# Squared-ReLU attention and a mixture of adapters on Trainium2: another engine for most output stores, two engines for the last ones, and a new order of work

## The chip, the cores and the metric

The kernel runs on one core of one Trainium2 chip. The metric is the device time of a whole execution in microseconds (us); lower is better. The core has five engines that run beside each other, each through its own queue in order: TensorE (PE in the profile; its weight loads are PEld), VectorE (DVE), ScalarE (ACT), GpSimd (POOL) and SyncE (SP, which here only issues DMAs). DMAs can be issued from SP, ACT and POOL.

## What is computed

```python
# q, k, v: (8, 12, 448, 64) float32
scores = q @ k.transpose(0, 1, 3, 2) / sqrt(64)
attn   = maximum(scores, 0) ** 2 / 448
x      = (attn @ v) brought to (8*448, 12*64) = (3584, 768)
logits = x @ w_gate                       # 8 experts
w      = softmax over the 2 largest logits of a row
out    = x + sum over these 2 experts e of  w_e * (x @ A[e]) @ B[e]     # A: 768 x 16, B: 16 x 768
```

The output has 3584 rows of 768 float32. There is no softmax over the scores, so score blocks need no maximum and no sum: a ReLU and a square.

## The kernel before

**Attention.** The heads go in quads: for each of 8 batches there are 3 quads of 4 heads (`QUADS`, line 19), and for each quad 7 blocks of 64 keys (`J`), so 168 units `n` in all. For each batch and quad, `load` (line 291) brings q, k and v into SBUF by two GpSimd DMAs each, casting float32 to bfloat16; `tp` (413) transposes q and k on TensorE and copies them out of PSUM (line 437, DVE). For each unit, `qk` (492) makes the scores, `relu` (514) takes them out of PSUM (line 523 on ACT, 525 on DVE), `sq` (533) squares two or three units at once on DVE (541), and `pv` (548) multiplies by v (558). When the 7 blocks of a quad are summed, `xt_copy` (576) casts the result into `xt`, the transposed x (587).

**Adapters.** The 3584 rows are 28 tiles of 128. Tiles go through the gate in groups of mostly three: `gate` (596) multiplies by A and w_gate (604), finds the two largest logits, the weights and the weighted `zp` on DVE with a sigmoid on ACT (641), transposes `zp` on TensorE (665) and copies it to `zT` (674). `outputs` (704) then makes each tile in two halves of 384 columns: a float32 matmul `zT` by B (722) in PSUM, the x part added, and one evacuation per half into the tile's buffer `osb`. For tiles 15 to 25 x comes from SP's DMA transposes (`turned`, 683, issued at line 690, six for a group) and is added on DVE during the evacuation (752). For the other tiles x is added on TensorE (717) and the evacuation is a copy on ACT or DVE (757). `st` (765) stores a finished tile by two SP DMAs of 64 rows (771). `osb` has 4 buffers, so a tile can only be written when the store of the tile four places ahead of it has landed.

**The order.** Nothing here is a loop on the chip. The function `build` (254) makes a list of operations, each with an estimate of its duration, the engines it may run on and a rank; `schedule` (114) plays them through as a list scheduler, with the durations, latencies and buffer counts written in the file, and the instructions are emitted in the order of its start times. Three tables steer it: `C` (weights and latencies), `RANKS` (shifts of single operations by their number in the list) and `ENGINES` (operations tied to one engine). The `deps` of an operation steer this order only; the waits on the chip come from the tiles and buffers that the instructions read and write. `Dma.land` (106) is the planner's idea of when a load lands. DMAs of POOL use eight completion semaphores in turn, those of SP and ACT together another eight, and each DMA waits for the one that used its semaphore before.

**The start.** `first` (304) loads the first k as float32 by SP and ACT, a first part of three blocks (`raw`) and the rest (`raw_rest`, through `rest`, 327), and casts them on DVE (`k0` at 344, `k1` at 346). The first q comes by POOL.

Of the kernel before, what the change touches and what calls it, by code (L numbers as in the profile page):

```python
# [14 lines left out]
J = 7  # L15
# [9 lines left out]
ZW = RE + E  # L25

# [5 lines left out]
def parts(*cuts):  # L32
# [6 lines left out]
    out_=-0.80943, zt_=6.6019, a12=(4, 7), late=6, merge_x=0, id2=2.6063, ocap=3, tboth=1, sqs=(2, 2, 3), xback=(15, 24), xblat=3.0, xbdur=0.7,  # L39
    slack=0.097634, switch=3.9663, third=7.3082, dve_relu=0.18096, relu_until=400, qk=-2.3217, sq=10,  # L40
# [3 lines left out]
POOLS = dict(qT=5, a1=C["a12"][0], a2=C["a12"][1], zp=2, zT=3, osb=4, w=3, q=5, k=5, v=7, xb=4)  # L44
# [4 lines left out]
    0: 20, 85: 141, 113: -42, 122: -40, 142: -8, 144: 17, 147: -27, 148: 84, 154: -31, 167: -104, 168:  # L49
    -23, 180: 36, 189: 32, 195: -52, 196: -21, 199: 18, 215: 4, 216: 110, 217: 47, 220: -25, 222: 9, 225:  # L50
    10, 231: 10, 233: -54, 234: -43, 238: -65, 245: 62, 267: 90, 286: 1, 295: 11, 321: 84, 334: 180, 336:
    45, 341: -33, 351: 3, 356: -10, 359: -9, 373: 5, 409: 4, 414: -23, 417: -24, 432: -12, 446: 69, 447:
    57, 452: 33, 454: 46, 467: -47, 491: -15, 496: 3, 508: -22, 519: 57, 521: -6, 529: -4, 562: 110, 563:
    35, 568: -23, 573: 18, 607: 2, 612: 30, 627: 9, 642: 3, 649: 6, 662: -7, 667: 21, 694: 20, 723: 2,
    746: -26, 769: -19, 805: 3, 807: 20, 814: -78, 815: -77, 826: 46, 834: 52, 837: 15, 841: -41, 842:
    -14, 924: -12, 925: -15, 926: 66, 930: -11, 931: -12, 947: 137, 950: 127, 963: -11, 968: -13, 970:
    -63, 983: 59, 986: -28, 989: 141, 994: 45, 1001: -57, 1031: 123, 1034: 106, 1044: -71, 1050: -94,
    1056: 34,
}
ENGINES = {  # L60
    100: "ACT", 108: "ACT", 141: "ACT", 142: "ACT", 196: "ACT", 218: "DVE", 234: "ACT", 280: "ACT", 315:
    "ACT", 330: "ACT", 337: "ACT", 360: "ACT", 432: "ACT", 566: "DVE", 664: "DVE", 759: "ACT", 780:
    "ACT", 1011: "ACT", 1012: "ACT",
# [18 lines left out]
class Op:  # L82
    def __init__(self, engs, dur, fn, deps=(), after=None, mode=None, kind="", take=(), give=(),
                 rank=0.0, banks=None, free=(), lat=None, ni=0):
        self.engs, self.fn, self.mode, self.kind = engs, fn, mode, kind
        self.dur = dur if isinstance(dur, dict) else dict.fromkeys(engs, dur)
        self.lat, self.ni = lat, ni
        self.deps = [d for d in deps if d is not None]
        self.after = after
        self.take, self.give, self.rank = take, give, rank  # L90
        self.want, self.free, self.banks = banks, free, None
        self.start = self.end = self.eng = None
        self.users = []
        self.missing = len(self.deps) + (after is not None)
        self.ready = 0.0
        for d in self.deps + [after] * (after is not None):
            d.users.append(self)


class Dma:  # L100
# [5 lines left out]
    def land(self, t, o):  # L106
        if o.engs[0] != "POOL":
            return t + o.lat
        for x in (t - o.dur["POOL"] / 2, t):
            self.free = max(self.free, x + 0.5) + o.mb / 2 / (0.27 if 4.5 < self.free < 13 else 0.4)  # L110
        return self.free + (1.5 if self.free < 5 else 2.1 if self.free < 11 else 2.7)


def schedule(ops, c=C):
# [70 lines left out]
    while left:  # L185
# [9 lines left out]
        for e in free:  # L195
# [12 lines left out]
            if o.kind == "load":  # L208
                o.end = dma.land(free[e], o)
            else:  # L210
                o.end = free[e] + (LAT[e] if o.lat is None else o.lat)
# [42 lines left out]
def build(k=None, c=C):  # L254
# [36 lines left out]
    def load(b, w, q, deps):  # L291
        nm = "qkv"[w]

        def fn():
            t = new(nm, (nm, b, q), [128, 2, S], BF16)
            for g in range(2):
                nc.gpsimd.dma_start(out=t[g * PH : g * PH + PH],  # L297
                                    in_=k.qkv[w][b, g, :, 2 * q : 2 * q + 2, :])

        o = op(("POOL",), 1.17, fn, deps=deps, kind="load", take=(nm, "lane"), give=("lane",))  # L300
        o.mb = 4 * S * 64 * 4e-6
        return o

    def first():
# [30 lines left out]
        for d in ds:  # L335
# [5 lines left out]
        kr = [op((e,), 0.75, lambda g=g: rest(g), kind="load", rank=-48.0, lat=2.4, after=aw if g else None, deps=[ob],  # L341
                 to=more if g else ops)
              for g, e in enumerate(("SP", "ACT"))]
        k0 = op(DVE, dve(2 * CUT * PH, 1.92), lambda: nc.vector.tensor_copy(k.k_first, k.raw), deps=ds + [ob],
                rank=-50.0)
# [67 lines left out]
    def tp(b, q):  # L413
# [34 lines left out]
        if (b, q) == (0, 0):  # L448
# [24 lines left out]
            return [[e1, *es] + [e2] * (j >= CUT) for j in range(J)]  # L473
        m = op(PE, 0.225, lambda: mm(m, 0), deps=[loaded[b, w, q] for w in range(1 + c.get("tboth", 0))], mode="64",
# [16 lines left out]

    def qk(n):
        b, u, q, j = order[n]
        x0, x1 = PARTS[b][u]
        w = x1 - x0

        def fn():
            t = T["qT", b, q]
            for sl in range(2):
                r = slice(sl * PH, sl * PH + PH)  # L500
                at = 0 if sl else 512 - w
                for g in range(2):
                    nc.tensor.matmul(  # L503
                        out=bank(o, sl)[g * PH : g * PH + PH, at : at + w],
                        lhsT=t[r, g, 1, j * PH : j * PH + PH], rhs=t[r, g, 0, x0:x1],
                        start=True, stop=True,
                    )

        o = op(PE, w / 2400 + 0.005, fn, mode="64", kind="qk", ni=8, deps=tp_ops[b, q][j],
               after=qk_ops.get(n - 1), banks=("s", 2), give=("qT",) if n == last_use[b, q] else (),  # L510
               rank=n + at("qk", n))
        return o
# [35 lines left out]
    def pv(n):  # L548
# [4 lines left out]
        def fn():  # L553
            vn = T["v", b, q]
            for g in range(2):
                r = slice(g * PH, g * PH + PH)
                for sl in range(2):
                    nc.tensor.matmul(  # L558
                        out=bank(head, g)[sl * PH : sl * PH + PH, :w],
                        lhsT=vn[r, sl, j * PH : j * PH + PH],  # L560
                        rhs=T["a2", g0][r, i, sl * w : sl * w + w],
                        start=(j == 0), stop=(j == J - 1),
                    )
# [7 lines left out]
        o = op(PE, w / 2400 + 0.003, fn, mode="64", kind="pv", ni=8, deps=wait, after=pv_ops.get(n - 1),  # L571
# [111 lines left out]
    def turned(tiles):  # L683
# [10 lines left out]
        for q in range(QUADS):  # L694
            for g in range(2):
# [4 lines left out]
                            lat=c["xblat"], to=more)  # L700
        for t in tiles:
            xb_of[t] = [[ts[do] for do in range(3 * h, 3 * h + 3)] for h in range(2)], t0, tiles[-1]

    def outputs(tl):
# [60 lines left out]
        def st():  # L765
            r = 0
            while r < 128:
# [3 lines left out]
                nc.sync.dma_start(out=k.out[b, j, p : p + m], in_=T["osb", tl][r : r + m, :])  # L771
                r += m

        op(("SP",), 0.8, st, deps=evs, give=("osb",), kind="store", lat=2.5)
# [13 lines left out]
    for i in range(len(tiles_of) + 2):  # L788
# [5 lines left out]
        if i == 4:  # L794
            sel_op = op(("POOL",), 1.5, sel_fn)
            a_load = op(("POOL",), 1.5, aw_fn, kind="load")
            a_load.mb = 0.4
            b_load = op(("POOL",), 0.7, b_fn, kind="load")
            b_load.mb = 0.4
# [4 lines left out]
    while t < NT:  # L804
        m = min(c.get("gsz", 3), NT - t)
        if NT - t == 4:
            m = 2
        if t == NT - 2:
            m = 1
# [133 lines left out]
```

## Time and profile before

| | before |
|---|---|
| median of 5 runs | 184.98 us (184.11 to 186.82) |
| the profiled execution | 183.92 us |
| its span, first to last instruction | 182.2 us |
| busy in the span: PE / DVE / ACT / POOL | 165.2 / 164.5 / 155.1 / 88.7 us |
| granted TensorE clock, mean | 0.997 |
| TensorE, start of its last matmul | 175.66 us |
| last evacuation, start | 176.4 us |
| last store DMA, issued | 177.88 us |
| store DMAs of SP (line 771), x56, issue to landing, median | 3.5 us |
| transposes of SP (line 690), x24, one issue, median | 1.25 us |
| load DMAs of POOL (line 297), one issue, mean | 0.62 to 0.63 us |

The profile is one execution, recorded by the hardware. Times inside it count from its first instruction. "Busy" is the time in which an engine had an instruction running; DMA issues on SP and ACT do not count as busy. A wait names what ended it. The profiled execution took 1.7 us more than its span, which lies outside the first and last instruction.

### The profile page before, as it was taken

The page shows a single profiled execution, that of the slowest core. Times are in us where ns is not written, and L with a number is a line of the kernel's source. Part 1 is how long each engine was busy: PE and PEld are TensorE (multiplying, and loading weights), DVE is VectorE, ACT ScalarE, POOL GpSimd, SP SyncE. Part 2 cuts the span into 40 slices and gives each one's busy share as a digit, 9 for nine tenths or more (in the row PEclk, how much of TensorE's full clock was granted, in tenths as well). Part 3 has the DMA queues.
Part 4 walks back from the last instruction along what each step waited for, and adds up shares of the span by engine and source line. Part 5 has one row for each costly group of instructions (what it writes and reads, how often), then busy time and mean ns, then how long its engine had stood idle before and what let it go on. Part 6 is the DMA issues. An engine that isn't in the chain of part 4 may idle for free.

```text
span 182.2 us, 7403 instructions
## 1 busy us (share of the span) xinstructions
PE 165.2 (91%) x3186; PEld 96.4 (53%) x3186; DVE 164.5 (90%) x260; ACT 155.1 (85%) x225; POOL 88.7 (49%) x153
## 2 busy tenths in 40 slices
PE   7777889698999999999999999999999999999960
PEld 2434667355565556565565555655665454656530
DVE  1289999999999999999999999999999999999750
ACT  3399989999999999999999999999999999941100
POOL 7999869889897586736835743720000000000000
PEclk9999999999999999999999999999999999999998
DMA  4999999999999999995999999999563973744785
GB/s 98 180 174 160 187 188 149 183 185 179 173 167 203 239 236 242 241 191 96 184 164 169 221 191 166 171 134 193 115 166 66 133 187 67 187 103 101 191 262 171
DMA packets 36018, 31.02 MB, mean 170 GB/s; under 512 B 13648, under 2 KB 32336, under 8 KB 35984
## 3 DMA queue, kind: packets, MB, share of 16 engines
q0 software_dynamic: 21712, 16.90, 65.2%
q1 hardware_dynamic: 13984, 13.41, 30.0%
q8 instruction: 25, 0.41, 0.8%
q10 hardware_dynamic: 288, 0.23, 0.5%
q14 instruction: 9, 0.07, 0.2%
HBM read 33.84 MB, written 11.01 MB: 246 GB/s over the span
## 4 chain that ended last, share of the span: by engine, by line
PE 52%; ACT 26%; DVE 10%; issue 6%; DMA 2%; DVEq 0%; POOL 0%; ACTq 0%; POOLq 0%
ACT a L523 22%; PE ps L722 17%; PE ps L503 12%; PE ps L558 10%; DVE a L541 5%; PE ps L604 3%; PE ps L423 3%; PE ps L717 3%; DMA q<-in_q_dram 2%; DVE xt L587 2%; PE ps L375 2%; DVE qT L437 2%; ACT xt L587 1%; ACT osb L757 1%; PE ps L665 1%
## 5 line engine op out<-in xcount | busy, mean ns | idle before, releaser
L523 ACT ACTIVATE a<-ps 128x896 bf16<-128x896 f32 x159 | 136.6, 972 | 2.0 <-PE ps L503 1.8
L541 DVE TENSOR_TENSOR a<-a 128x1792 bf16<-128x1792 bf16 (+1 forms) x72 | 88.7, 1250 | 0.8 <-ACT a L523 0.7
L503 PE MATMUL ps<-qT 64*64 64x448 bf16 x672 | 60.0, 367 | 5.5 <-ACT a L523 3.8
L722 PE MATMUL ps<-B,zT 128*128 128x384 f32 x112 | 46.7, 512 | 0.1
L558 PE MATMUL ps<-a,v 64*64 64x448 bf16 x672 | 42.1, 350 | 1.4 <-ACT a L523 0.7
L503 PEld LDWEIGHTS <-qT 64*64 64x64 bf16 x672 | 24.0, 105 | 35.9 <-issue 27.1
L297 POOL DMA_DIRECT2D v<-in_v_dram x48 | 29.0, 619 | 21.1 <-PE ps L503 10.6
L297 POOL DMA_DIRECT2D q<-in_q_dram x48 | 29.4, 625 | 6.8 <-PE ps L423 2.1
L297 POOL DMA_DIRECT2D k<-in_k_dram x46 | 28.0, 630 | 3.3 <-PE ps L503 1.8
L558 PEld LDWEIGHTS <-v 64*64 64x64 bf16 x672 | 21.6, 106 | 11.8 <-issue 4.6
L437 DVE COPY qT<-ps 128x1792 bf16<-128x1792 bf16 x23 | 25.0, 1087 | 0.6 <-PE ps L423 0.4
L722 PEld LDWEIGHTS ps<-B,zT 128*128 128x128 f32 x112 | 17.6, 191 | 5.1 <-issue 1.0
L587 DVE CAST xt<-ps 128x448 bf16<-128x448 f32 x26 | 15.5, 622 | 0.9 <-PE ps L558 0.8
L604 PE MATMUL ps<-awg,xt 128*128 128x136 bf16 x168 | 13.4, 224 | 0.1
L423 PEld LDWEIGHTS <-q 64*64 64x64 bf16 x672 | 10.3, 111 | 4.8 <-issue 1.9
L604 PEld LDWEIGHTS <-xt 128*128 128x128 bf16 x168 | 10.2, 98 | 4.7 <-issue 4.0
L752 DVE TENSOR_TENSOR osb<-ps,xb 128x384 f32<-128x384 f32 x22 | 11.9, 556 | 0.8 <-DMA out_dram<-osb 0.4
L587 ACT CAST xt<-ps 128x448 bf16<-128x448 f32 x22 | 12.2, 590 | 0.3 <-PE ps L558 0.3
L717 PE MATMUL ps<-identb,xt 128*128 128x128 bf16 x102 | 11.5, 221 | 0.3 <-ACT a L523 0.2
L423 PE MATMUL ps<-identb,q 64*64 64x64 bf16 x672 | 10.0, 195 | 1.8 <-DMA q<-in_q_dram 1.3
L757 ACT COPY osb<-ps 128x384 f32<-128x384 f32 x22 | 11.5, 536 | 0.2
L717 PEld LDWEIGHTS <-xt 128*128 128x128 bf16 x102 | 6.6, 97 | 8.6 <-issue 7.7
(47 smaller groups left out, 95.7 us busy)
## 6 DMA issues: line engine op xcount, KB each, us to landing
out_dram<-osb SPq DMA_DIRECT2D x56, 192.0 KB, 3.5
q<-in_q_dram POOLq DMA_DIRECT2D x48, 112.0 KB, 4.9
v<-in_v_dram POOLq DMA_DIRECT2D x48, 112.0 KB, 5.0
k<-in_k_dram POOLq DMA_DIRECT2D x46, 112.0 KB, 5.1
B<-in_moe_B_dram POOLq DMA_DIRECT2D x1, 384.0 KB, 6.2
xb<-xt SPq DMA_TRANSPOSE x24, 2.9
a_raw<-in_moe_A_dram POOLq DMA_DIRECT2D x1, 192.0 KB, 5.0
raw_rest<-in_k_dram ACTq DMA_DIRECT2D x1, 128.0 KB, 4.6
```

The lines of the kernel that those rows point to most:

```text
L297: nc.gpsimd.dma_start(out=t[g * PH : g * PH + PH], in_=k.qkv[w][b, g, :, 2 * q : 2 * q + 2, :])
L423: nc.tensor.transpose(k.ps_b[sl * PH : sl * PH + PH, o.banks[g], (w * J + j) * PH : (w * J + j) * PH + PH], source(w, j)[r, sl], k.identb[ ...
L437: nc.vector.tensor_copy(t.rearrange("p g w x -> p g (w x)"), k.ps_b[:, m.banks[0] : m.banks[0] + 2, : 2 * S])
L503: nc.tensor.matmul(out=bank(o, sl)[g * PH : g * PH + PH, at : at + w], lhsT=t[r, g, 1, j * PH : j * PH + PH], rhs=t[r, g, 0, x0:x1], start ...
L523: nc.scalar.activation(out, flat(qk_ops[n], w), ACTF.Relu, scale=k.relu_scale)
L541: nc.vector.tensor_mul(a2, T["a1", g0], T["a1", g0])
L558: nc.tensor.matmul(out=bank(head, g)[sl * PH : sl * PH + PH, :w], lhsT=vn[r, sl, j * PH : j * PH + PH], rhs=T["a2", g0][r, i, sl * w : sl ...
L587: evac(w, lambda cp, g=g: cp(k.xt[:, g * QUADS + q, b * S + x0 : b * S + x1], bank(src, g)[:, :w]), deps=[pv_ops[n]], free=[(src, g)], ran ...
L604: nc.tensor.matmul(out=bank(zops[0])[:, t * ZW : t * ZW + ZW], lhsT=k.xt[:, do, 128 * tiles[t] : 128 * tiles[t] + 128], rhs=k.awg[:, do, : ...
L717: nc.tensor.matmul(out=out(h)[:, x * 128 : x * 128 + 128], lhsT=k.xt[:, 3 * h + x, c0 : c0 + 128], rhs=k.identb, start=(x == 0), stop=Fals ...
L722: nc.tensor.matmul(out=out(h)[:, :W], lhsT=T["zT", g0][:, zi], rhs=k.B[:, h * W : h * W + W], start=xb is not None, stop=True, skip_group_ ...
L757: cp(T["osb", tl][:, h * W : h * W + W], out(h)[:, :W])
```

## The change

- A table `STORES` gives the stores of tiles 6 to 22 to POOL and those of tiles 24 and 26 to ACT; the other tiles but the last stay with SP. The last tile, 27, is stored in halves of 384 columns: the first by SP once the first half is evacuated, the second by ACT after the second. A half takes two DMAs, as a whole tile did.
- The planner's operations for `raw_rest` (`kr`) depend on the cast `k0` and no longer on `ob`, and stand behind it in the list.
- The planner's numbers change: a tile's store 1.4 (POOL 1.05) where it was 0.8, a transpose 1.35 with latency 1.4 where it was 0.7 with 3.0; `Dma.land` now also models stores and transposes. `xb`, the transposed x, has 3 buffers where it had 4.
- `slack`, `switch`, `third` and `dve_relu` in `C` are new, and `RANKS` and `ENGINES` are replaced by other tables, so the order of all work is another.
- The k tile gets 64 more columns, and there are new functions `turn_qk` and `qk_turned` for batches from `bx` on. `bx` is 8 and there are 8 batches, 0 to 7, so they are never called, and the columns stay unused. `gl=(2, 1)` gives the group sizes that the code had.

```diff
+STORES = {**dict.fromkeys(range(6, 23), "POOL"), 24: "ACT", 26: "ACT"}
...
-    ..., xback=(15, 24), xblat=3.0, xbdur=0.7,
-    slack=0.097634, switch=3.9663, third=7.3082, dve_relu=0.18096, ...
+    ..., xback=(15, 24), xblat=1.4, xbdur=1.35, bx=8, gl=(2, 1), tqk=-25.0, tqlat=2.0,
+    slack=0.09816, switch=4.3786, third=6.0149, dve_relu=0.47201, ...
-POOLS = dict(..., v=7, xb=4)
+POOLS = dict(..., v=7, xb=3)
...
     def land(self, t, o):
+        if o.kind != "load":
+            self.free = max(self.free, t - o.dur[o.engs[0]] + 0.6) + o.mb
+            return max(self.free + 1.3, t + o.lat)
...
-        kr = [op((e,), 0.75, lambda g=g: rest(g), kind="load", rank=-48.0, lat=2.4, after=aw if g else None, deps=[ob],
+        k0 = op(DVE, dve(2 * CUT * PH, 1.92), lambda: nc.vector.tensor_copy(k.k_first, k.raw), deps=ds + [ob],
+                rank=-50.0)
+        kr = [op((e,), 0.75, lambda g=g: rest(g), kind="load", rank=-48.0, lat=1.6, after=aw if g else None, deps=[k0],
                  to=more if g else ops)
               for g, e in enumerate(("SP", "ACT"))]
-        k0 = op(DVE, dve(2 * CUT * PH, 1.92), lambda: nc.vector.tensor_copy(k.k_first, k.raw), deps=ds + [ob],
-                rank=-50.0)
...
-        def st():
+        def st(e, c1=0, c2=2 * W):
...
-                nc.sync.dma_start(out=k.out[b, j, p : p + m], in_=T["osb", tl][r : r + m, :])
+                {"SP": nc.sync, "ACT": nc.scalar, "POOL": nc.gpsimd}[e].dma_start(
+                    out=k.out[b, j, p : p + m, c1:c2], in_=T["osb", tl][r : r + m, c1:c2])
                 r += m
 
-        op(("SP",), 0.8, st, deps=evs, give=("osb",), kind="store", lat=2.5)
+        def store(e, es, **kw):
+            half = "fn" in kw
+            o = op((e,), 1.05 if e == "POOL" else 1.4, kw.pop("fn", lambda: st(e)), deps=es, kind="store", lat=1.9, **kw)
+            o.mb = (1.25 if e == "POOL" else 1.5) / (1 + half)
+
+        if tl < NT - 1:
+            store(STORES.get(tl, "SP"), evs, give=("osb",))
+        else:
+            store("SP", evs[:1], fn=lambda: st("SP", 0, W))
+            store("ACT", evs[1:], fn=lambda: st("ACT", W, 2 * W), give=("osb",), to=more)
```

## The prediction, made before the changed kernel was run

> **What bounds the kernel now.** I first read the busy times by stretch: the body (attention, with the outputs of the tiles that are complete), the tail after the last attention matmul, and the end after the last matmul.
>
> ```profile
> core 0: us, PE busy (x) PEld busy (x) DVE busy (x) ACT busy (x) POOL busy (x), PEclk, DMA share, GB/s
> 8.30:163.10 154.80, 146.52 (x3056) 86.06 (x3049) 151.34 (x218) 150.93 (x215) 81.53 (x137) 1.00 1.02 171
> 163.10:176.20 13.10, 12.87 (x71) 7.71 (x71) 10.44 (x34) 2.07 (x7) 0.00 (x0) 1.00 0.66 171
> 176.20:182.20 6.00, 0.00 (x0) 0.00 (x0) 0.77 (x2) 0.00 (x0) 0.00 (x0) 0.92 0.59 199
> ```
>
> In the body DVE and ACT are both idle for under 4 us of 154.8, so their summed work sets its length. In the tail PE is busy for 12.87 of 13.1 us and ACT is nearly idle. The last 6.0 us hold two evacuations, a store and the closing waits. Next, the timeline of the last 15 us, where SP is the engine to watch:
>
> ```profile
> 163.48 5.08 SPq L690 DMA_TRANSPOSE xb<-xt  x4
> ...
> 168.65 9.98 SPq L771 DMA_DIRECT2D out_dram<-osb  x14
> ...
> 173.99 2.15 PE L722 MATMUL ps<-B,zT 128*128 128x384 f32 x6
> 175.02 1.02 DVE L757 COPY osb<-ps 128x384 f32<-128x384 f32 x2 [1.30 <-PE ps L722]
> 175.96 1.01 DVE L752 TENSOR_TENSOR osb<-ps,xb 128x384 f32<-128x384 f32 x2
> ```
>
> Fourteen store DMAs are seven tiles, a quarter of the output. SP comes to them only after four transposes, then issues them nearly end to end; at 175.02 DVE starts four evacuations in a row, though the first of these tiles had its matmuls before. The timeline of SP alone gives the last issue:
>
> ```profile
> 177.88 0.76 SPq L771 DMA_DIRECT2D out_dram<-osb  x1
> ```
>
> The waits of the whole run show what POOL is held by, and that the head waits for q, once:
>
> ```profile
> POOL v L297 <- PE ps L503: 10.6, 5, 4.8
> ...
> PE ps L423 <- DMA q<-in_q_dram: 1.3, 1, 1.3
> ...
> DVE osb L752 <- DMA out_dram<-osb: 0.4, 1, 0.4
> ```
>
> POOL mostly waits for buffers that matmuls free (us in total, times, longest), not for DMAs: loads run ahead. The start, again from the timeline:
>
> ```profile
> 1.56 0.62 ACTq L309 DMA_DIRECT2D raw_rest<-in_k_dram  x1
> 1.56 0.82 SPq L309 DMA_DIRECT2D raw_rest<-in_k_dram  x1
> ...
> 3.17 0.23 DVE L340 CAST identb<-identf 128x128 bf16<-128x128 f32 x1 [2.04 <-POOL identf masks.py:199]
> ```
>
> The planner made `raw_rest` depend on that cast, which ends at 3.40, yet both DMAs went out at 1.56.
>
> **What the Trainium skill says.** "DMA: Bandwidth & Descriptors", section "Issuing engines are not separate DMA queues": all DMAs run on the same 16 engines, and issuing from several engines only saves the sequencer's issue time. The trace agrees as far as it goes: stores of SP took 5.3 us to land between 60 and 123 us, beside POOL's loads, and 3.1 us between 123 and 160. So POOL and ACT bring issue time, no bandwidth. "SBUF — State Buffer", section "Who interferes with whom": DVE in a 2-port mode and GpSimd lock each other out of a shared port, and that delays GpSimd's descriptors. The trace shows no price: POOL's load issues between 60 and 123 us span 590 to 658 ns beside a DVE that is busy 61.52 of 63 us.
>
> **The change part by part.** The sum is made against the profiled execution: 183.92 us, of which 182.2 is span.
>
> *Stores of tiles 6 to 22 by POOL.* They add 17 x 2 = 34 DMAs of about 0.6 us (line 297's issues), 20.4 us. From the times of SP's stores, six of these tiles (6 to 11) come before the last load at 120.5 us: 12 x 0.6 = 7.2 us, against 63 - 36.0 = 27 us in which POOL is idle between 60 and 123. A store that waits for its evacuation holds the loads behind it, and POOL's eight semaphores are shared. But q of the thirteenth quad is issued at 49.5 and used at 75.7, and later ones lead by 26 us or more, so a few us are hidden. If that cover were gone, PE would wait for q; I find no place. After 123 us POOL is empty. Landing: POOL's loads take about 5 us, so I reckon 5 us for its stores. `osb` is written again four tiles later; from 145 to 163 us that distance is over 10 us. Only tile 22 is close: evacuated at 168.4, landed near 174, needed near 175.0. Cost 0.
>
> *Freed SP.* In the stretch of the trace before 163 us SP stood at stores waiting for evacuations, with transposes queued behind: it waited from 161.7 until 162.28 and issued until 163.39 before the transpose of 163.48. Without that the last six start about 1 us earlier and land near 169.4 instead of 170. That and earlier free `osb` remove DVE's wait of 0.4 us at 171.1; but PE sets this stretch, and its matmuls start 0.325 us apart with 0.2 us of gaps there. Gain 0.2 us.
>
> *The last evacuations.* The tile copied at 175.02 had its first half ready near 174.2; its buffer belongs to a store issued at 169.92 and 170.52, landing about 3.5 us later, late because SP was. With free buffers, and any copy on ACT, DVE meets the last two matmul pairs on time: the last one starts at 175.66, ends at 176.15, and an evacuation of 0.55 ends at 176.7 instead of 176.97. Gain 0.3 us.
>
> *The last store.* Now from 176.97: SP is free 0.2 us late, its second DMA goes at 177.88, lands near 181.0 (3.1 us), and closing waits take it to 182.16: 5.2 us. After: ACT issues at once, its second DMA 0.65 us after the evacuation, each of half the bytes; landing between 2.6 (the shortest of line 771) and 3.1; closing 1.15. That is 4.4 to 4.9; I take 4.6. Gain 0.6 us. ACT's stores of tiles 24 and 26 (four issues, 2.4 us) lie in a tail where ACT is busy 2.07 of 13.1 us. Behind them stand sigmoids (641) and `zT` copies (674), for which PE waits; if such a store waits for a late DVE evacuation, that is lost: 0 to 1 us. I take 0.
>
> *`raw_rest`.* If the new dependence reached the chip, its issue would go from 1.56 to about 4.6 (the cast ends at 4.62), landing at 4.6 + 4.8 = 9.4 instead of near 6.4; the relu of the fourth unit could lose 0.5 us, and q, which shares the DMA engines with it, could gain at most the 1.3 us that PE waits for it. Bounds -1.3 to +0.5. But the trace of before shows that such a dependence makes no wait, and these DMAs stay second on their queues. I take 0.
>
> *The new order.* The work is the same: 56 halves, 168 units. What can differ is how many output halves are left for the tail. Now 14 are: tiles 21 to 27. Tiles 24 to 27 need the last batch; 21 to 23 don't. Moving those three before 163.1 takes 6 x 0.66 = 4.0 us of PE out of the tail (2.15 us for three halves, less overlap) and puts 6 x 0.556 = 3.3 us of evacuation into a body where ACT and DVE are full: 1.7 us if the two share it. So at best -2.3, and a group more in the tail +2.3. I take -0.8, a third of the gain: the planner's new durations (transpose 1.35, store 1.4) agree with the trace (1.25; 1.2 for two issues), while the old ones (0.7, 0.8) placed SP's work too tightly. `xb` with three buffers costs nothing, with four groups of transposed tiles (15, 18, 21, 24) and the first long used.
>
> Sum: 0 - 0.2 - 0.3 - 0.6 + 0 - 0.8 = -1.9 us: 182.0 for the profiled execution. The median stands 1.06 us above that execution, so 183.1; I forecast 183.0.
>
> **Rivals.** One per cent of 184.98 is 1.85 us, about what can be told from no change.
> A (0.5), the sum above: 183.0, itself within 181.8 to 184.2.
> B (0.2), the order also brings the group of 21 to 23 before the end of attention: the firm 1.1 and the full 2.3 us: 181.6. For it: the gate of this group ran at 157.8, soon after its x was complete near 155. Against: DVE is full there.
> C (0.15), no change: the end gains its 1.1 us and the order gives it back in the body, or the closing landing is the same: 184.0 to 185.0. For it: DVE and ACT have under 4 us of idle time there to win.
> D (0.15), slower: the order leaves one more group of three, 18 to 20, to the tail, +2.3, less the firm 1.1, and `osb` then waits for POOL's slower landings, up to 1 us more: PE stops, since at 2 x 0.66 = 1.3 us a tile four buffers turn over in 5.2 us, under the 5.6 us of issue and landing. It decides once ten tiles stand in the tail: 186.2 to 187.2.
>
> **Numbers.** Faster by over 1% (under 183.1): 0.3 of A and all B, 0.5. Within: 0.2 of A and C, 0.35. Slower: D, 0.15. The range of 180.5 to 186.2 takes in A, C, B with up to 1 us more from q, and D's lower end.
>
> **What would show it.** Right: the last store's issue within 0.7 us of the last evacuation and 4.4 to 4.9 us from there to the end; `raw_rest` still issued at 1.56; the first relu near 8.26; at most seven tiles' halves after the last attention matmul; POOL's loads leading by over 20 us. Wrong: `raw_rest` issued after 4.6; a wait of DVE on out_dram in the tail; ACT's sigmoids held behind its stores; attention ending later than 164.

## The result and the profile after

| | before | after |
|---|---|---|
| median of all runs | 184.49 us (79 runs, 182.66 to 187.32) | 185.74 us (44 runs, 183.96 to 190.70) |
| middle half of the runs | 183.94 to 185.2 us | 185.2 to 186.8 us |
| the profiled execution | 183.92 us | 184.48 us |
| its span | 182.2 us | 182.6 us |
| last attention matmuls end, about | 163.1 us | 165.6 us |
| halves of output tiles that follow them | 14 | 13 |
| last evacuation ends | 176.97 us | 177.94 us |
| from there to the end of the span | 5.2 us | 4.67 us |

The ratio of the two kernels' times is 1.0059, with an interval of 1.0042 to 1.0076. Runs more than 1.5% above the fastest of their own kernel are left out of ratios here, so a ratio says too little of a kernel whose times spread widely; the medians of all runs are given beside it. The change made the kernel a little slower, by 0.6% to 0.7%, where the prediction expected it to become 1.1% faster. (That was reckoned from the median of five runs, 184.98; over 79 runs the kernel before stands 0.5 us lower.)

First the busy times of the changed kernel, by the same stretches and columns as in the prediction:

```profile
8.30:163.10 154.80, 144.91 (x3030) 83.92 (x3022) 149.74 (x217) 151.39 (x215) 96.74 (x165) 1.00 1.05 170
163.10:176.20 13.10, 13.06 (x92) 7.74 (x92) 11.15 (x35) 2.34 (x8) 3.14 (x6) 1.00 0.75 185
176.20:182.60 6.40, 1.07 (x6) 0.41 (x4) 1.12 (x2) 0.00 (x0) 0.00 (x0) 0.89 0.58 188
```

In the body PE and DVE have each lost 1.6 us of busy time in the same 154.8 us. The last line shows that six matmuls still run after 176.2, where before there were none. The loss lies in the body, and finer stretches find it. Here are 120 to 140 us, first of the kernel before, then of the changed one:

```profile
120.00:140.00 20.00, 19.63 (x381) 11.74 (x369) 19.52 (x34) 19.64 (x31) 1.10 (x2) 1.00 0.89 143
```

```profile
120.00:140.00 20.00, 18.92 (x425) 10.94 (x417) 18.53 (x29) 18.69 (x28) 4.41 (x8) 1.00 1.20 164
```

All three computing engines stand idle for over 1 us in these 20 us, where each was idle for under half a microsecond. If other work had merely been put there, some engine should still be full. The last column but one is the mean share of time that the 16 DMA engines have packets under way (it counts overlapping packets, so it can pass 1): it rose from 0.89 to 1.20. The start times of single ReLUs, of the 168 counted from 0, tell where the lag grows:

| ReLU number | 112 | 120 | 136 | 144 | 160 |
|---|---|---|---|---|---|
| before, us | 107.92 | 115.40 | 130.40 | 137.72 | 152.05 |
| after, us | 108.08 | 116.19 | 131.73 | 139.50 | 154.88 |

What the prediction said of the start and the end can be read directly. The two loads of `raw_rest`, from the changed kernel's timeline:

```profile
1.56 0.83 SPq L316 DMA_DIRECT2D raw_rest<-in_k_dram  x1
1.57 0.65 ACTq L316 DMA_DIRECT2D raw_rest<-in_k_dram  x1
```

They still go out at 1.56 us, and the first ReLU is at 8.22 (8.26 before). The end, from the same timeline:

```profile
176.16 3.04 ACTq L844 DMA_DIRECT2D out_dram<-osb  x4
...
176.44 0.56 DVE L828 COPY osb<-ps 128x384 f32<-128x384 f32 x1 [0.31 <-PE ps L793]
177.02 1.25 SPq L844 DMA_DIRECT2D out_dram<-osb  x2
177.38 0.56 DVE L828 COPY osb<-ps 128x384 f32<-128x384 f32 x1 [0.38 <-PE ps L793]
```

Both evacuations wait for matmuls and none for an `osb`. SP stores the first half while DVE copies the second, and ACT issues the last DMA at 178.48, 0.54 us after the last evacuation.

Last, two DMA groups of the page that changed more than expected, line 690 of before and 760 of after, with the median of issue to landing:

```profile
xb<-xt SPq DMA_TRANSPOSE x24, 2.9
```

```profile
xb<-xt SPq DMA_TRANSPOSE x24, 4.6
```

### The profile page after: what moved, and what is told of

The parts are those of the page before. It is cut to its first block, busy times and chain, and to the rows that moved or that the text cites. A ratio compares the mean times of both kernels' runs of the same rounds, so it can differ in the third digit from the quotient of the medians.

```text
span 182.6 us, 7418 instructions
## 1 busy us (share of the span) xinstructions
PE 164.9 (90%) x3186; PEld 94.7 (52%) x3186; DVE 164.0 (90%) x260; ACT 155.8 (85%) x225; POOL 107.0 (59%) x187
## 4 chain that ended last, share of the span: by engine, by line
PE 52%; ACT 23%; DVE 14%; issue 5%; DMA 2%; POOL 0%; ACTq 0%; DVEq 0%; POOLq 0%
ACT a L584 20%; PE ps L793 17%; PE ps L564 12%; PE ps L628 11%; DVE a L602 8%; PE ps L674 3%; PE ps L788 3%; DVE qT L444 2%; PE ps L430 2%; DMA q<-in_q_dram 2%; DVE xt L657 2%; PE ps L382 2%; PE ps L735 1%; ACT osb L828 1%; ACT xt L657 1%
## 5 line engine op out<-in xcount | busy, mean ns | idle before, releaser
L564 PE MATMUL ps<-qT 64*64 64x448 bf16 x672 | 60.7, 366 | 5.0 <-ACT a L584 3.8
L628 PE MATMUL ps<-a,v 64*64 64x448 bf16 x672 | 44.0, 351 | 2.0 <-ACT a L584 1.1
L844 POOL DMA_DIRECT2D out_dram<-osb x34 | 18.3, 545 | 38.6 <-DVE osb L823 22.6
L657 ACT CAST xt<-ps 128x448 bf16<-128x448 f32 x25 | 13.6, 580 | 2.5 <-PE ps L628 2.5
L657 DVE CAST xt<-ps 128x448 bf16<-128x448 f32 x23 | 13.8, 621 | 1.5 <-PE ps L628 1.5
L430 PE MATMUL ps<-identb,q 64*64 64x64 bf16 x672 | 10.6, 196 | 2.6 <-DMA q<-in_q_dram 1.2
L674 PE MATMUL ps<-awg,xt 128*128 128x136 bf16 x168 | 12.0, 223 | 0.0
L674 PEld LDWEIGHTS <-xt 128*128 128x128 bf16 x168 | 10.1, 98 | 3.1 <-issue 2.8
L828 ACT COPY osb<-ps 128x384 f32<-128x384 f32 x20 | 10.3, 519 | 1.1 <-PE ps L793 1.1
```

The source lines that it names most:

```text
L430: nc.tensor.transpose(k.ps_b[sl * PH : sl * PH + PH, o.banks[g], (w * J + j) * PH : (w * J + j) * PH + PH], source(w, j)[r, sl], k.identb[ ...
L564: nc.tensor.matmul(out=bank(o, sl)[g * PH : g * PH + PH, at : at + w], lhsT=t[r, g, 1, j * PH : j * PH + PH], rhs=t[r, g, 0, x0:x1], start ...
L628: nc.tensor.matmul(out=bank(head, g)[sl * PH : sl * PH + PH, :w], lhsT=vn[r, sl, j * PH : j * PH + PH], rhs=T["a2", g0][r, i, sl * w : sl ...
L657: evac(w, lambda cp, g=g: cp(k.xt[:, g * QUADS + q, b * S + x0 : b * S + x1], bank(src, g)[:, :w]), deps=[pv_ops[n]], free=[(src, g)], ran ...
L674: nc.tensor.matmul(out=bank(zops[0])[:, t * ZW : t * ZW + ZW], lhsT=k.xt[:, do, 128 * tiles[t] : 128 * tiles[t] + 128], rhs=k.awg[:, do, : ...
L844: {"SP": nc.sync, "ACT": nc.scalar, "POOL": nc.gpsimd}[e].dma_start(out=k.out[b, j, p : p + m, c1:c2], in_=T["osb", tl][r : r + m, c1:c2])
```

## What stopped TensorE

The chain that ended last, between 110 and 145 us of the changed kernel, holds 0.61 us of "issue" at 126.72: time in which TensorE waited for nothing that the profile shows. The timeline there:

```profile
126.18 0.55 PE L628 MATMUL ps<-a,v 64*64 64x448 bf16 x7
...
127.33 0.13 PEld L628 LDWEIGHTS <-v 64*64 64x64 bf16 x5 [1.04 <-issue]
127.34 0.56 PE L628 MATMUL ps<-a,v 64*64 64x448 bf16 x5 [0.61 <-issue]
...
128.12 0.92 ACT L584 ACTIVATE a<-ps 128x896 bf16<-128x896 f32 x1 [0.70 <-PE ps L564]
```

Weight loads and matmuls stop together in the middle of a group of identical attention matmuls, and then ACT waits 0.70 us for scores. No semaphore, buffer or DMA of the program is involved. The next clue is in the page's table of DMA queues and its first table:

```profile
PE 164.9 (90%) x3186; PEld 94.7 (52%) x3186; DVE 164.0 (90%) x260; ACT 155.8 (85%) x225; POOL 107.0 (59%) x187
...
q8 instruction: 25, 0.41, 1.0%
```

The profile thus lists fetches of the core's own instructions among its DMA packets, and counts their time against the same 16 DMA engines: 25 packets in 0.41 MB, 16.4 KB each. TensorE ran 3186 + 3186 = 6372 instructions, and 6372 / 25 = 255: one packet is 256 instructions of TensorE. In the kernel before the row is:

```profile
q8 instruction: 25, 0.41, 0.8%
```

The last column is the time of the packets as a share of 16 engines over the span, so one packet took about 0.9 us before (0.008 x 16 x 182.2 / 25) and about 1.2 us after. Numbering everything recorded of TensorE in a trace from 0 in order of time (matmuls, weight loads and the few semaphore and drain instructions), one can list every step of over 0.45 us from one to the next, after 9 us, where the second of the two waits for no semaphore:

```
kernel   time us (length of the step us)                            index mod 256
before   61.87 (0.48)  120.46 (0.56)                                193 193
after    62.78 (0.99)  120.59 (0.53)  127.33 (0.96)  133.81 (0.47)  193 193 193 193
e1       61.96 (0.79)  120.56 (0.69)                                193 193
e2       120.78 (1.34) 128.63 (2.06)                                193 193
e3       62.40 (1.50)                                               193
e4       none
e5       29.62 (0.89)                                               193
e6       61.87 (0.82)  120.85 (1.07)  135.71 (0.63)                 193 193 193
e7       15.13 (0.58)                                               193
e8       25.50 (0.70)  61.54 (1.10)                                 193 193
e9       63.36 (1.57)                                               193
e10      104.11 (1.30) 123.87 (1.08)  130.62 (0.97)                 193 193 193
e11      27.11 (0.92)  121.07 (0.69)                                193 193
e13      26.59 (0.70)  62.14 (0.61)                                 193 193
```

(e1 to e13 are the experiments below; e12 follows there.) All stand at the same place in a piece of 256, over different lines of code, and each step ends 1.28 to 1.58 us after an instruction packet did. The reading that fits is that TensorE stops when it has used up what was fetched and the next piece is late. The changed kernel lost 2.95 us in such steps and the kernel before 1.04. That difference of 1.9 us is most of the 2.5 us by which attention ended later.

Two rows of the table warn against reading too much into one trace. e2, with all stores on SP, has 3.4 us of stops, more than the changed kernel, and e4, with tiles 6 to 22 on POOL, has none. So late fetches also come without POOL's stores. The traces of e2 and e10 are of the longest execution of their kernel (186.01 and 186.94 us), that of e4 is of the shortest of its own (183.5). Over all the traces the stops go with the time: executions under 184 us have 0 to 1.8 us of them, and those over 185 us have 2.5 us or more, but for e5, which has another cause.

## The experiments

Three theories stood at the start: that the stores on POOL cost the time, somewhere in the body; that the new order costs it; that the last stores do. That late instruction fetches are how POOL's stores cost it was formed from the traces of e1 to e7.

**Stores and order apart (e1 to e4).** e1 is the old order with the new stores, e2 the new order with all stores on SP, e3 the old order with only the last stores changed, e4 the old order with only tiles 6 to 22 on POOL. In the old order both halves of tile 27 are issued where its store stood.

```diff
 e1, e3, e4 (from before; st takes an engine and columns, as in the change)
+STORES = {**dict.fromkeys(range(6, 23), "POOL"), 24: "ACT", 26: "ACT"}   # e1
+STORES = {24: "ACT", 26: "ACT"}                                          # e3
+STORES = dict.fromkeys(range(6, 23), "POOL")                             # e4, tile 27 whole
 e2 (from after)
-                {"SP": nc.sync, "ACT": nc.scalar, "POOL": nc.gpsimd}[e].dma_start(
+                nc.sync.dma_start(
...
-            store("SP", evs[:1], fn=lambda: st("SP", 0, W))
-            store("ACT", evs[1:], fn=lambda: st("ACT", W, 2 * W), give=("osb",), to=more)
+            store("SP", evs[:1], fn=lambda: None)
+            store("ACT", evs[1:], fn=lambda: st("SP"), give=("osb",), to=more)
```

> The order of the kernel before, word for word, with the stores of the change (6 to 22 by POOL, 24 and 26 and half of 27 by ACT). Theory O (the new order of work costs what the change lost, the stores gain): faster than before by about 0.9 us, ratio 0.995, attention ending at 163 as before. Rival P (the stores on POOL hold loads or landings back, the order is neutral): slower than before by about 1.1 us, ratio 1.006, attention ending near 165.5.

> The new order with every store issued by SP, the last tile whole. Theory O: slower than before by 1.1 us and what the stores gain, 1.6 to 2.5 us in all, ratio 1.009 to 1.014, all three compute engines idle together near 126 and 134 us as in the changed kernel. Rival P: as fast as before or up to 0.5 us faster, without these idle times.

> The order before, tiles 24 and 26 by ACT, 27 in halves by SP and ACT, all others by SP. Theory O: faster than before by 0.5 to 0.9 us (ratio 0.995 to 0.997), from the end alone: 4.6 us from the last evacuation to the end where it was 5.2. Rival P: the same. If the last tile evacuated is not 27 but 25, as in the order before, the gain can be as small as 0.

> The order before, tiles 6 to 22 stored by POOL, the others by SP as before. Theory O: between 0 and 0.5 us faster than before, since SP's transposes and last stores come sooner. Rival P: 1 to 2 us slower, with PE waiting for q or v, or VectorE waiting for out_dram.

| | median us (range, runs) | before beside it | ratio (interval) |
|---|---|---|---|
| e1 | 186.38 (183.76 to 189.9, 22) | 184.55 | 1.0042 (1.0009 to 1.0074) |
| e2 | 184.45 (182.89 to 186.01, 22) | 184.55 | 0.9999 (0.9971 to 1.0027) |
| e3 | 184.56 (182.87 to 185.85, 22) | 184.55 | 0.9987 (0.9959 to 1.0014) |
| e4 | 185.95 (183.5 to 192.36, 14) | 184.55 | 0.9986 (0.9946 to 1.0026) |

The theories of the order and of the last stores fell. The new order alone costs nothing and brings nothing, and neither do the last stores alone. Both kernels with tiles 6 to 22 on POOL have medians 1.4 to 1.8 us above the kernel before, and a wide spread: the middle half of e4 lies between 184.4 and 187.2, that of the kernel before between 184.0 and 185.0. The cost is in POOL's stores, and it differs from one execution to the next; the trace of e4, of its shortest execution, shows no stop. What the expectation of e4 named as the way of the cost is not in that trace: after the head, TensorE waits for no q or v, and VectorE for no store.

In e3 the forecast gain of 0.5 to 0.9 us did not come. In its trace the time from the last evacuation to the end fell to 4.26 us, but that evacuation ended 1.7 us after the last matmul (0.8 in the kernel before), because DVE still had to wait for buffers, as two lines of its timeline show:

```profile
175.36 1.02 DVE L758 COPY osb<-ps 128x384 f32<-128x384 f32 x2 [1.30 <-DMA out_dram<-osb]
...
177.69 1.02 DVE L753 TENSOR_TENSOR osb<-ps,xb 128x384 f32<-128x384 f32 x2 [1.30 <-DMA out_dram<-osb]
```

With the backlog of tiles 15 to 22 still on SP, splitting the last store didn't help.

**The wait that was not there (e5).** The prediction took `raw_rest` at 0, since no wait existed, and gave -1.3 to +0.5 us if it had. Here it exists: `raw` and `raw_rest` share one buffer, so the two loads must wait for the first cast.

```diff
+            k.raw_rest = k.one.tile([128, 2, (J - CUT) * PH], F32, name="raw_rest", tag="raw")
+            rest(0)
+            rest(1)
...
-    h.raw = const.tile([128, 2, CUT * PH], F32)
-    h.raw_rest = const.tile([128, 2, (J - CUT) * PH], F32)
+    h.one = ctx.enter_context(tc.tile_pool(name="one", bufs=1))
+    h.raw = h.one.tile([128, 2, (J - CUT) * PH], F32, name="raw", tag="raw")[:, :, : CUT * PH]
```

> The kernel before, with raw and raw_rest in one buffer, so that the load of the rest really waits for the cast of the first part (issue near 4.6 us, not 1.56). If that wait is dear: slower by up to 0.5 us, because the fourth block of k comes later. If it only clears the way for q: the first relu starts up to 1 us earlier and the kernel is faster by as much. Both theories of the change (order, stores) expect nothing of it, since neither traced kernel has this wait.

It took 186.94 us (186.6 to 188.23, 6 runs) beside 184.43: ratio 1.0163 (1.0123 to 1.0203). The gain that I had allowed came: q was there sooner, and the first ReLU ran at 7.05 instead of 8.26. But then, in the waits between 5 and 20 us:

```profile
DVE k_rest L352 <- DMA raw_rest<-in_k_dram: 4.7, 1, 4.7
...
PE ps L429 <- DVE k_rest L352: 4.4, 1, 4.4
```

ReLU number 8 came at 17.02 instead of 13.95. The wait also cost clock: TensorE's granted clock in e5 was 0.50 from 9.7 to 16.5 us; in the kernel before it was 1.00 from 10.5 on. The changed kernel has no such wait, so the term of 0 stands; the bound of +0.5 did not.

**Which of POOL's stores (e6, e7).** In e6 POOL issues the stores of tiles 6 to 14 between 87 and 136 us; the last load lands at 131, and the transposes begin at 114. In e7 POOL issues those of 15 to 22 between 143 and 169 us, beside the last transposes and no loads.

```diff
+STORES = dict.fromkeys(range(6, 15), "POOL")     # e6, otherwise as e4
+STORES = dict.fromkeys(range(15, 23), "POOL")    # e7
```

> The order before, tiles 6 to 14 stored by POOL (beside the loads and up to about 131 us), all others by SP. Theory P, that POOL's stores cost, in its first form (P1: stores and loads hold each other back on POOL's queue and semaphores): median 1 to 1.9 us above before and a wide spread, as with 6 to 22 (185.95, up to 192.4). In its second form (P2: from 139 us on, the stores' late landings or the slowed transposes hold the output tiles): like before, 184.5 with a spread to about 187.

> The order before, tiles 15 to 22 stored by POOL (from about 145 us on, when no loads are left), all others by SP. P1: like before, 184.5. P2: median 1 to 1.9 us above before with a wide spread. If both halves cost about half each, neither form alone is right.

e6: 187.22 us (185.45 to 188.75, 6 runs) beside 184.43, ratio 1.0188 (1.0134 to 1.0242). e7: 183.83 (182.68 to 187.01, 17 runs), ratio 0.9981 (0.9954 to 1.0009). The cost is in tiles 6 to 14: 2.8 us for 18 DMAs that POOL has time to issue. The size is rough, since e6 has six runs; e1 and e4, which move the same tiles and more, stand at 1.8 and 1.4. In the trace of e6 the time is 1.5 us above that of the kernel before, and its stops are 1.5 us longer in sum. The timeline of e6 shows a stop that also stands in the kernel before, grown from 0.56 to 1.07 us:

```profile
120.85 0.31 PE L424 MATMUL ps<-identb,k 64*64 64x64 bf16 x14 [0.88 <-issue]
...
121.28 1.09 DVE L438 COPY qT<-ps 128x1792 bf16<-128x1792 bf16 x1 [0.96 <-PE ps L424]
...
121.46 0.92 ACT L524 ACTIVATE a<-ps 128x896 bf16<-128x896 f32 x1 [0.40 <-PE ps L504]
```

In the kernel before the same copy waited less, and ACT did not wait:

```profile
120.89 1.09 DVE L437 COPY qT<-ps 128x1792 bf16<-128x1792 bf16 x1 [0.45 <-PE ps L423]
121.07 0.94 ACT L523 ACTIVATE a<-ps 128x896 bf16<-128x896 f32 x1
```

A second stop, of 0.63 us at 135.71, is new. Why there: the busy times from 126 to 140 us of before and then of e6 (same order of work, same instructions on TensorE):

```profile
126.00:140.00 14.00, 14.00 (x310) 8.96 (x299) 13.96 (x28) 13.93 (x22) 0.00 (x0) 1.00 0.59 114
```

```profile
126.00:140.00 14.00, 13.41 (x293) 8.43 (x286) 13.74 (x28) 13.12 (x20) 2.18 (x5) 1.00 1.23 172
```

The DMA share is twice as high. On SP these stores stood in one queue with the transposes, and on POOL they can run beside them. How late a fetch is can be read against the moment at which TensorE issues instruction 196 of a piece, about when the packet starts where nothing delays it. The two packets that start between 124 and 134 us start this long after it: 3.8 and 0.7 us in the kernel before, 5.3 and 4.8 in e6, 4.2 and 4.1 in the changed kernel. In e4 they are 4.4 and 4.0 us late and no stop follows, so in these runs a fetch that starts about 4 us late is at the edge. A piece lasts 6.5 us on average in the body of the kernel before (154.8 us for 3056 + 3049 instructions, 23.8 pieces), less where many short transposes follow each other.

**Transposes and stores together (e8, e9), and two mixtures (e10, e11).** e8 and e9 leave out SP's 24 transposes, so the tiles that use them have zeros added in place of x: e8 with tiles 6 to 14 on POOL, e9, in the same way, with all stores on SP. e10 is the changed kernel with tiles 6 to 14 back on SP. e11 is the old order with 15 to 22 on POOL and the last stores as in the change.

```diff
 e8, e9 (from before)
         def turn(do):
-            if ("xb", t0) not in T:
-                new("xb", ("xb", t0), [128, 3, DO, 128], BF16)
-            nc.sync.dma_start_transpose(out=T["xb", t0][:, :n, do, :],
-                                        in_=k.xt[:, do, 128 * t0 : 128 * (t0 + n)])
+            T["xb", t0] = k.xb0
 e10 (from after)
+EMIT = {t: "SP" for t in range(6, 15)}
-                {"SP": nc.sync, "ACT": nc.scalar, "POOL": nc.gpsimd}[e].dma_start(
+                {"SP": nc.sync, "ACT": nc.scalar, "POOL": nc.gpsimd}[EMIT.get(tl, e)].dma_start(
 e11 (from before, otherwise as e1)
+STORES = {**dict.fromkeys(range(15, 23), "POOL"), 24: "ACT", 26: "ACT"}
```

> As the run with tiles 6 to 14 stored by POOL (187.22, 2.8 us over before), but SP's 24 transposes are left out: the adds of tiles 15 to 25 read a buffer of zeros. Theory F (TensorE starves because its own instructions, fetched through the same DMA engines in pieces of 16 KB, come late where loads, POOL's stores and transposes run together, 113 to 137 us): the 2.8 us shrink to under 1, measured against the same kernel without transposes and with SP's stores, and no gap of TensorE without a semaphore appears after 100 us. Rival P1 (POOL's stores hold the loads behind them, and TensorE waits for data): the 2.8 us stay.

> The kernel before with the transposes left out in the same way. The baseline for the run above. Theory F: 184.5 or up to 0.5 us faster, since its own small gap at 120.5 us (0.37) goes, and a narrower spread than before. P1: 184.5.

> The changed kernel with its order, but tiles 6 to 14 stored by SP; 15 to 22 stay with POOL, the last ones with ACT and SP. If POOL's early stores are what the change lost: 184.0 to 184.4, the same as before or up to 0.3% faster, with a spread to 186.5 at most. If the new order or the last stores lost it: 185.7 as the changed kernel.

> The order before, tiles 15 to 22 stored by POOL, 24 and 26 and half of 27 by ACT, all else by SP: the parts that cost nothing so far. From the run with 15 to 22 alone (183.83) and the shorter end (0.4 us between the profiles of before and of the first experiment): 183.3 to 183.8, ratio about 0.995, faster than both kernels. If ACT's stores hold the zT copies: 184.5.

| | median us (range, runs) | before beside it | ratio (interval) |
|---|---|---|---|
| e8 | 184.67 (182.85 to 189.06, 22) | 184.75 | 0.9978 (0.9949 to 1.0007) |
| e9 | 184.46 (182.29 to 186.95, 22) | 184.75 | 0.9968 (0.9941 to 0.9996) |
| e10 | 184.61 (182.97 to 186.94, 14) | 184.75 | 0.9980 (0.9942 to 1.0018) |
| e11 | 183.99 (182.72 to 186.12, 22) | 184.75 | 0.9966 (0.9937 to 0.9995) |

Without transposes the move of tiles 6 to 14 costs 0.2 us (e8 against e9), with them 2.8. So these stores on POOL cost nothing that can be told unless the transposes are there. That the loads are needed too rests on e7 alone, where stores on POOL meet transposes but no loads, and cost nothing. e9 did not get the narrower spread that was expected of it: its middle half is 1.3 us wide, as that of the kernel before beside it. The busy times of e8 for 126 to 140 us:

```profile
126.00:140.00 14.00, 14.00 (x298) 8.58 (x290) 13.89 (x30) 13.93 (x22) 1.77 (x4) 1.00 0.25 65
```

TensorE is full again, at a DMA share of 0.25. Both e8 and e9 still stop once near 62 us (1.10 and 1.57 us), where loads run. e10 brings the changed kernel back to the time of the kernel before. e11 is below the kernel before by 0.8 us in median, with an interval that just leaves out no change (so does that of e9, which does less work), and 1.8 us below the changed kernel. Most of that is e7's part (0.6 us in median); what the new last stores add to it is too small to be told.

**Moving the pieces, and no stores at all (e12, e13).** If a stop belongs to the fetch, 64 more instructions at the start must move it to 64 instructions earlier in the work. e12 is the changed kernel with 32 more matmuls on zeros at the start (36 small ones, and 4 warming ones fewer). e13 is the old order in which the rows of tiles 6 to 14 are never stored.

```diff
 e12 (from after)
-            for _ in range(SPIN):
+            for _ in range(SPIN - 4):
                 nc.tensor.matmul(k.ps[:, 7, :], lhsT=k.zeros[:, :128], rhs=k.zeros, start=True, stop=True)
+            for _ in range(36):
+                nc.tensor.matmul(k.ps[:, 7, :8], lhsT=k.zeros[:, :128], rhs=k.zeros[:, :8], start=True, stop=True)
 e13 (from before)
-        op(("SP",), 0.8, st, deps=evs, give=("osb",), kind="store", lat=2.5)
+        op(("SP",), 0.8, lambda: None if 6 <= tl <= 14 else st("SP"), deps=evs, give=("osb",), kind="store", lat=2.5)
```

> The changed kernel with 64 more TensorE instructions in the idle start (four of the eight warm-up matmuls left out, 36 tiny ones put in). Theory F (TensorE stops at the borders of its instruction pieces): all stops without a semaphore stay at the 193rd of every 256 instructions, counted anew, so they fall 64 instructions earlier in the program; the time changes by whatever the new places cost, between 184.5 and 187, spread still wide. Rival (the stops belong to places in the program, data or buffers that the trace does not name): they stay at the same matmuls, at the 257th less 192, that is at 1 of 256, and the time stays 185.7.

> The order before, SP stores all tiles but 6 to 14, which are not stored at all (those rows of the output stay unwritten). If POOL's store packets are the cost: 184.0 to 184.5, no slower than before. If SP's transposes, no longer held apart by its stores, are the cost: 185.5 to 187.2, and stops of TensorE between 120 and 137 us as with POOL's stores.

e12 took 188.97 us (187.5 to 190.76, 6 runs) beside 184.45, ratio 1.0208 (1.015 to 1.0266), more than the 184.5 to 187 expected. The traced execution is the longest of the six. Its stops are at 49.42 (0.87 us), 67.83 (0.53) and 129.00 (4.33), all at index 193 of the pieces counted anew. (Two more steps, at 130.04 and 130.82 at indices 202 and 203, follow the big one.) The big one, from its timeline:

```profile
129.00 0.50 PE L790 MATMUL ps<-identb,xt 128*128 128x128 bf16 x3 [3.97 <-issue]
...
130.93 0.48 ACT L830 COPY osb<-ps 128x384 f32<-128x384 f32 x1 [4.67 <-PE ps L795]
...
133.03 1.09 DVE L588 TENSOR_SCALAR a<-ps 128x896 bf16<-128x896 f32 x1 [5.46 <-PE ps L566]
```

Its fetch packet started 5.5 us late by the same measure. So in this execution the same work, shifted against the pieces, loses more in one place than the changed kernel in its four stops. The places moved with the count, as the theory of the fetch said and its rival did not: where the stops fall is a matter of counting. That their length depends on what the DMA engines have to do just then fits the late packet, and is not shown by itself. About 0.9 us of e12's loss has another cause: its head ran later by that much (q landed at 7.24).

e13 took 185.2 us (183.17 to 186.45, 22 runs) beside 184.45, ratio 1.0046 (1.0017 to 1.0075), though it does less. Neither of the two expected times came. Its one trace, of 184.51 us, has no stop after 100 us, and its ReLU number 144 is at 137.74, as before (137.72), so in that execution the body lost nothing. What it lost lies in the tail: the last matmul ends at 176.17 as before, but the last evacuation at 177.58 instead of 176.97, after a wait for a store:

```profile
175.27 1.02 DVE L758 COPY osb<-ps 128x384 f32<-128x384 f32 x2 [1.51 <-DMA out_dram<-osb]
```

Leaving SP's queue without these stores can thus cost up to 0.8 us by itself, by a way other than late fetches as far as the one trace shows. How much of e6's 2.8 us is of that kind, and how much needs POOL's packets, stays open.

## Why the prediction was wrong

*"Stores of tiles 6 to 22 by POOL ... Cost 0."* This is the step that failed: the cost put at 0. The covers that it named held: POOL's loads still lead, and its new waits are for evacuations, as the first two store rows of the changed kernel's waits show.

```profile
POOL out_dram L844 <- DVE osb L823: 22.6, 7, 8.1
POOL out_dram L844 <- ACT osb L828: 12.6, 3, 4.9
```

After the head, PE never waited for q, k or v. The measured cost is 2.8 us for tiles 6 to 14 alone, and in median 1.4 to 1.8 for 6 to 22. That the early stores on POOL cost this beside SP's transposes is shown (e6 against e7 and e8; e10 takes the loss away). How they cost it is in part argued. The step left out a user of the DMA engines that no line of the kernel issues: TensorE's instruction fetch. Between 112 and 137 us loads, transposes and these stores now run at once, fetches come late, and TensorE stops; the traces of the changed kernel and of e6 show it, and e12 shows that such stops belong to the pieces. But e2 has such stops with SP's stores, so POOL's stores can at most make them longer or more frequent, and how often they come over many executions was not measured. The prediction did use "DMA: Bandwidth & Descriptors", section "Issuing engines are not separate DMA queues", in the right sense, that POOL brings no bandwidth. It did not ask what issuing from SP alone had done: it kept these stores and the transposes in one queue. That section's other remark, that several issuing engines only save issue time, does not cover this case: here it cost time. The same page, in "Queues, rings and completion order", says that each DMA engine goes round its queue rows packet by packet, so a fetch packet would wait its turn behind others. The late fetches agree with it (0.7 us became 4.8), but no run here shows a single engine's turn.

Both signs stood in the profile of before: the row "q8 instruction" in the DMA queues, and this stop of its timeline, in a stretch with transposes, loads and stores:

```profile
120.46 0.20 PEld L423 LDWEIGHTS <-k 64*64 64x64 bf16 x14 [0.48 <-issue]
120.46 0.31 PE L423 MATMUL ps<-identb,k 64*64 64x64 bf16 x14 [0.37 <-issue]
```

A wait for "issue" in a run of short matmuls looks like the queue's own pace. It was the only one of its size in that stretch, and the prediction passed over it.

*The new order, taken as -0.8.* Measured -0.1 (e2), with an interval around no change: this term was too large, and is the second part of the miss. The tail did lose one half-tile, 13 instead of 14, far less than the three tiles that rival B wanted; attention alone does not show a gain.

*Freed SP -0.2, last evacuations -0.3, last store -0.6.* The last store was right: from the last evacuation to the end 4.67 us, within the 4.4 to 4.9 given, a gain of 0.5. DVE's waits for `osb` in the tail are gone, as forecast. The last evacuation gained 0.15 us where 0.3 was forecast: 0.82 us lay between the ends of the last matmul and of the last evacuation before, 0.67 after. The last stores alone give 0.0 (e3); with tiles 15 to 22 on POOL all three parts give 0.8 us in median (e11, 0.6 by its ratio), of the 1.1 forecast for them. The changed kernel had them too, and lost more in the body.

*`raw_rest`, taken as 0.* Right: no wait. Its upper bound was wrong: a real wait costs 2.5 us (e5), since not only the fourth unit but a chain of cast, transposes and copies stands behind it, and TensorE's clock fell during the wait.

*The rivals.* The slower rival D had the place wrong: no more tiles stood in the tail, and `osb` did not wait. The listed sign that the prediction would be wrong, attention ending later than 164, did come, at 165.6. The slower end was reached by a mechanism that no rival named. Within the range, and within 1% of before, is where the time fell; the direction was wrong.

What stays open: how much of the 2.8 us goes through late fetches and how much through another way, and how often each stop occurs, since each trace is one execution of a kernel whose executions differ by several us.

## What to carry to other kernels

Before moving DMAs to another queue, ask what the old queue kept apart: here stores on a third queue, beside loads and transposes, went with later fetches of what the core loads for itself, its instructions. A TensorE stop that is put down to "issue", with the other engines soon idle too, can be checked by counting: if such stops stand at one place modulo 256 instructions of TensorE, soon after an instruction packet, a late fetch is the likely cause. Look then at what the DMA engines carry at that moment. Move only the transfers that lie outside the crowded stretch (here tiles 15 to 22: e11, 183.99 us beside 184.75, a small gain).

## What the runs showed of the hardware that was not expected

- TensorE's instructions come by DMA in packets of 16.4 KB, 256 instructions each, and TensorE stood for 0.5 to 4.3 us where one was late. Every such stop in the table, and the three of e12, stands at index 193 of a piece, 1.2 to 1.6 us after the end of a packet.
- A long stop costs twice, by the time and by the clock after it. "TensorE: Matmul & The Clock Gate", section "What's actually happening", says that TensorE's clock falls to half after an idle window of about 3.4 us. e12 agrees: after the stop of 4.3 us, which began at 124.66, the clock fell at 128.2. The busy times of 131 to 134 us:

```profile
131.00:134.00 3.00, 3.00 (x36) 1.45 (x34) 0.97 (x1) 2.13 (x3) 1.11 (x2) 0.50 0.99 160
```

  The granted clock is 0.50, and full again only at about 135, 6 us after work resumed. The 2.06 us stop of e2 left it at 1.00.
- Landing of an SP transpose varies: between 100 and 130 us its median was 6.3 us in the kernel before and 8.1 us in the changed one, and the longest rose from 7.3 to 11.3. POOL's stores alone do not set it: it was 8.3 in e2, with all stores on SP, and 4.7 in e13, with fewer stores.
